# Windowed attention moved from VectorE products to masked band products on TensorE, beside a state-space scan, on one core

## Chip, cores and metric

One core of a Trainium2 chip. The metric is the time of one execution in microseconds (us): the median of the executions, lower is better. The profile's span, from the first to the last instruction, is about 2 us shorter than the time. Some executions fall into a slower state, over 1.5% above the fastest of the same kernel; ratios use fast ones alone, medians and ranges of times use all.

## The reference, cut to what matters

The output joins two independent halves, A and B, each for 2,048 positions and 448 features.

```python
def _A_ref(x, ...):                     # a diagonal complex recurrence over 2048 steps
    ...
    for t in range(L):
        h = Lam_bar[None, :] * h + Bu[:, t, :]
    ...
    y = 2.0 * jnp.einsum("blp,dp->bld", hseq, Cmat).real + x * Dskip

def _B_ref(x, wqkv, wo):                # 16 heads of 28; each query sees 8 keys, 2 apart
    qkv = (x @ wqkv).reshape(B, S, 3, H, Dh)...
    idx = pos[:, None] - jnp.arange(8) * 2          # masked where negative
    logits = jnp.einsum("bhsd,bhswd->bhsw", q, k[idx]) * Dh ** -0.5
    attn = softmax(logits)
    return jnp.einsum("bhsw,bhswd->bhsd", attn, v[idx]).reshape(B, S, D) @ wo
```

## The kernel before

Part A is untouched by the change: weights and transposes, a first level of products, a second level of seven steps, and a last phase of 16 steps (`coA`, `coB`, two evictions `ht`, `y_ps`, eviction `ya`). Part B before the change holds 16 positions in each of 128 partitions, so that a key 2w positions back lies in the same partition, and does the whole attention on VectorE.

```python
def prep(self):                                   # x is loaded plain and turned by TensorE
    for j in range(T):
        for k in range(KT):
            nc.tensor.transpose(pt[:, k, :], self.x_sb[:, j, k*KP:(k+1)*KP], self.ident[:])
        nc.scalar.copy(self.xT[:, :, j, :], pt[:])
    ...
def attention(self):
    for w in range(W):                            # scores: 8 products over 7168 elements, then sums
        V.tensor_tensor(pr[:], qd..., kd[:, :, off:off+T, :]..., op=ALU.mult)
        V.tensor_tensor(pr[:, 0:14], pr[:, 0:14], pr[:, 14:28], op=ALU.add)
        ...
    ...                                           # max, exp (ScalarE), sum, divide
    for (j0, j1) in ((0, 12), (12, 16)):
        for w in range(W):                        # values: product and sum
            V.tensor_tensor(tmp..., aa, vv, op=ALU.mult)
            V.tensor_tensor(acc..., acc..., tmp..., op=ALU.add)
        self.tail(j0, j1)                         # transposes, output projection, store
...
a.loads_params(); b.loads(); a.loads(); b.prep(); a.setup()
b.qk_proj(); b.v_proj(); a.setup_c(); a.setup_weights(); b.loads2()
a.main()                                          # TensorE, ScalarE
b.attention()                                     # VectorE: runs beside a.main()
```

## Time and profile before

| | before |
|---|---|
| time | 212.96 us, median of 2 (212.83 to 213.09) |
| span | 211.4 us |
| VectorE busy | 181.0 us (86%) |
| TensorE busy | 160.4 us (76%) |
| TensorE's granted clock, mean | 0.96 |

From the page of the kernel before: busy time of the engines (DVE is VectorE, PE TensorE), three rows of the span in 40 slices (each digit the busy share of 5.3 us in tenths; PEclk is the granted clock), and the shares of the chain that ended last.

```profile
PE 160.4 (76%) x1709; PEld 117.4 (56%) x1709; DVE 181.0 (86%) x197; ACT 100.2 (47%) x193; POOL 28.1 (13%) x35
PE   0004999999997799999995763998888883297773
DVE  0359998888929999999999996999999999999950
PEclk9999999999999999999999998599999999569999
PE 46%; DVE 33%; ACT 8%; DMA 6%; issue 3%; SPq 2%; ACTq 0%; DVEq 0%
```

VectorE is above 90% in nearly all slices from 63 us to the end, and TensorE is busy in the same slices. The chain runs through TensorE first and through VectorE after it.

The same kernel by stages. Columns: stretch in us, its length, then the busy time of TensorE, TensorE's weight loads, VectorE, ScalarE and GpSimd, the clock, the DMA share and GB/s.

```profile
18.50:62.60 44.10, 43.82 (x268) 25.64 (x269) 36.85 (x63) 20.76 (x35) 26.95 (x16) 1.00 0.54 137
123.70:176.80 53.10, 42.42 (x404) 28.02 (x401) 50.22 (x26) 27.56 (x55) 0.00 (x0) 0.94 0.31 90
176.80:211.40 34.60, 19.80 (x128) 11.42 (x128) 27.14 (x33) 8.52 (x16) 0.00 (x0) 0.85 0.17 57
```

From 18.5 us, when x has landed, to 62.6 TensorE does part B's projections without a hole. Part A's last phase, 123.7 to 176.8, lies wholly beside VectorE's softmax and value products (50.2 of 53.1 us busy). Only the 34.6 us after it are attention alone.

Two of the groups of VectorE instructions that the change removes (count, then busy us and mean ns of one):

```profile
L129 DVE TENSOR_TENSOR prod<-qd,kd 128x7168 bf16<-128x7168 bf16 x8 | 30.7, 3840 | 0.1
L165 DVE TENSOR_TENSOR pv_tmp<-attn,vd 128x5376 bf16<-128x5376 bf16 (+1 forms) x14 | 28.3, 2021 | 0.3
```

### The profile page before, as it was taken

What the parts mean: (1) busy time and instruction counts of PE and PEld (TensorE: products, weight loads), DVE (VectorE), ACT (ScalarE), POOL (GpSimd) and SP (SyncE); (2) the same over time, 40 slices, a digit from 0 to 9 for tenths busy, and PEclk for the clock granted to TensorE, in tenths of its full rate; (3) what the DMA queues carried; (4) which work ended last, traced back from release to release, by engine and by line L of the source; (5) the groups of instructions that cost most, each with busy time, mean ns of one, the idle gap of its engine ahead of it and who ended that gap; (6) DMA issues with size and microseconds to landing.
All of it is one profiled execution on the core that took longest, in us unless ns stands there. A gap on an engine that the chain in (4) does not pass through costs nothing.

```text
span 211.4 us, 4117 instructions
## 1 busy us (share of the span) xinstructions
PE 160.4 (76%) x1709; PEld 117.4 (56%) x1709; DVE 181.0 (86%) x197; ACT 100.2 (47%) x193; POOL 28.1 (13%) x35
## 2 busy tenths in 40 slices
PE   0004999999997799999995763998888883297773
PEld 0003765555567799999994652565555551154441
DVE  0359998888929999999999996999999999999950
ACT  2053792002689993344337796344455541024432
POOL 2000899991000000000000000000000000000000
PEclk9999999999999999999999998599999999569999
DMA  1599940485508515422231011134354411012212
GB/s 0 103 351 289 244 108 0 108 192 161 212 2 209 95 47 171 164 106 90 87 118 59 3 43 43 47 110 129 92 137 126 112 43 43 0 43 72 83 65 87
DMA packets 23836, 22.17 MB, mean 105 GB/s; under 512 B 11786, under 2 KB 23114, under 8 KB 23562
## 3 DMA queue, kind: packets, MB, share of 16 engines
q1 hardware_dynamic: 20231, 20.32, 32.9%
q10 hardware_dynamic: 3587, 1.59, 3.2%
q8 instruction: 13, 0.21, 0.5%
q14 instruction: 5, 0.04, 0.1%
HBM read 11.36 MB, written 7.34 MB: 88 GB/s over the span
## 4 chain that ended last, share of the span: by engine, by line
PE 46%; DVE 33%; ACT 8%; DMA 6%; issue 3%; SPq 2%; ACTq 0%; DVEq 0%
PE qkv_ps L95 18%; DVE pv_tmp L165 13%; DVE acc L167 10%; PE l1A L392 7%; DMA xb_sb<-in_B_x_dram 6%; PE l1B L392 5%; PE wo_ps L188 3%; PE pt_x L80 3%; DVE oT_sb L185 2%; PE pt_x L415 2%; DVE o_nat L169 2%; ACT Bcat L379 2%; PE l1A L397 1%; PE l1A L399 1%; ACT Ccat L250 1%
## 5 line engine op out<-in xcount | busy, mean ns | idle before, releaser
L95 PE MATMUL qkv_ps<-wqkv_p,xbT_sb 112*128 112x448 bf16 x192 | 40.1, 361 | 0.0
L129 DVE TENSOR_TENSOR prod<-qd,kd 128x7168 bf16<-128x7168 bf16 x8 | 30.7, 3840 | 0.1
L165 DVE TENSOR_TENSOR pv_tmp<-attn,vd 128x5376 bf16<-128x5376 bf16 (+1 forms) x14 | 28.3, 2021 | 0.3
L95 PEld LDWEIGHTS <-xbT_sb 112*128 112x128 bf16 x192 | 18.8, 100 | 15.5
L392 PEld LDWEIGHTS <-Bcat 112*128 112x128 bf16 x448 | 26.2, 98 | 0.0
L167 DVE TENSOR_TENSOR acc<-acc,pv_tmp 128x5376 bf16<-128x5376 bf16 (+1 forms) x12 | 24.3, 2024 | 0.3
L80 PE MATMUL pt_x<-ident,xb_sb 128*112 128x128 bf16 x64 | 7.8, 266 | 18.8 <-DMA xb_sb<-in_B_x_dram 18.5
L483 ACT CAST ya<-y_ps 128x448 bf16<-128x448 f32 x16 | 8.5, 531 | 23.4 <-issue 18.8
L191 ACT CAST yb<-wo_ps 128x448 bf16<-128x448 f32 x16 | 8.5, 532 | 23.3 <-PE wo_ps L188 23.3
L80 PEld LDWEIGHTS <-xb_sb 128*112 128x112 bf16 x64 | 7.5, 173 | 21.1 <-DMA xb_sb<-in_B_x_dram 18.5
L402 ACT CAST ht<-l1A 128x512 bf16<-128x512 f32 x16 | 9.4, 587 | 19.2 <-issue 17.0
L119 ACT CAST vd<-qkv_ps 128x448 bf16<-128x448 f32 x16 | 8.4, 536 | 20.8 <-PE qkv_ps L95 20.7
L392 PE MATMUL l1A<-xaT_sb,Bcat 112*128 112x128 bf16 x256 | 18.1, 219 | 0.0
L188 PE MATMUL wo_ps<-wo_p,oT_sb 112*128 112x448 bf16 x64 | 15.0, 382 | 3.8 <-DVE oT_sb L185 3.7
L131 DVE TENSOR_TENSOR prod<-prod 128x3584 bf16<-128x3584 bf16 x8 | 16.2, 2025 | 0.3
L343 POOL TENSOR_TENSOR Mmat<-Dm,Scat 128x896 bf16<-128x896 f32 x7 | 11.6, 1688 | 19.3 <-DVE Scat L335 19.3
L392 PE MATMUL l1B<-xaT_sb,Bcat 112*128 112x128 bf16 x192 | 14.2, 219 | 0.0
L81 ACT COPY xbT_sb<-pt_x 112x512 bf16<-112x512 bf16 x16 | 8.8, 587 | 7.3 <-PE pt_x L80 7.3
L184 PE MATMUL pt_o<-ident,o_nat 128*112 128x128 bf16 x64 | 5.8, 244 | 8.3 <-DVE o_nat L169 8.3
L113 DVE TENSOR_SCALAR qd<-qkv_ps 128x448 bf16<-128x448 f32 x16 | 10.0, 625 | 2.1
L188 PEld LDWEIGHTS <-oT_sb 112*128 112x128 bf16 x64 | 6.0, 103 | 10.1 <-DVE oT_sb L185 5.0
L469 PEld LDWEIGHTS <-ident 128*128 128x128 bf16 x112 | 11.3, 101 | 0.0
(206 smaller groups left out, 360.9 us busy)
## 6 DMA issues: line engine op xcount, KB each, us to landing
hs<-ht SPq DMA_DIRECT2D x16, 224.0 KB, 1.9
hin<-hs SPq DMA_DIRECT2D x16, 224.0 KB, 2.7
xb_sb<-in_B_x_dram SPq DMA_DIRECT2D x1, 1792.0 KB, 12.3
xa_sb<-in_A_x_dram SPq DMA_DIRECT2D x1, 1792.0 KB, 7.9
out_dram<-ya SPq DMA_DIRECT2D x16, 112.0 KB, 1.7
out_dram<-yb SPq DMA_DIRECT2D x16, 112.0 KB, 1.7
kd<-kd ACTq DMA_DIRECT2D x1, 1372.0 KB, 9.1
vd<-vd SPq DMA_DIRECT2D x1, 1372.0 KB, 9.4
```

Of the source, the lines that this page charges most:

```text
L80: nc.tensor.transpose(pt[:, k, :], self.x_sb[:, j, k * KP:(k + 1) * KP], self.ident[:])
L95: nc.tensor.matmul(ps[:].rearrange("p d h -> p (d h)"), lhsT=self.xT[:, k, j, :], rhs=self.wp[:, k * 3 + which].rearrange("p d h -> p (d h)"),
L113: V.tensor_scalar(self.qd[:, :, j, :], ps[:], scale, None, op0=ALU.mult)
L129: V.tensor_tensor(pr[:], qd[:].rearrange("p d j h -> p d (j h)"), kd[:, :, off:off + T, :].rearrange("p d j h -> p d (j h)"), op=ALU.mult)
L131: V.tensor_tensor(pr[:, 0:14], pr[:, 0:14], pr[:, 14:28], op=ALU.add)
L165: V.tensor_tensor(tmp[:, :, 0:n, :], aa, vv, op=ALU.mult)
L167: V.tensor_tensor(acc[:, :, j0:j1, :], acc[:, :, j0:j1, :], tmp[:, :, 0:n, :], op=ALU.add)
L188: nc.tensor.matmul(ps[:], lhsT=oT[:, kt, j, :], rhs=self.wo_p[:, kt, :], start=(kt == 0), stop=(kt == KT - 1))
L343: eng.tensor_tensor(out_tile, Dm[:].unsqueeze(1).unsqueeze(1).to_broadcast([NCH, n, 2, PL]), scal.unsqueeze(3).to_broadcast([NCH, n, 2, PL ...
L392: nc.tensor.matmul(reg(m), lhsT=self.Bcat[:, k, m, :], rhs=self.xT[:, k, j, :], start=(k == 0 and m in (0, MA)), stop=(not has_prev and k ...
L402: nc.scalar.copy(ht[:, 0:MA, :], psA[:])
L469: nc.tensor.matmul(reg(m), lhsT=ident[:], rhs=hin[:, m, :], start=(m in (0, MA)), stop=False, skip_group_check=True)
```

## The change

The intent: scores and values become matrix products on TensorE instead of VectorE's 135 us of products, which go. For 114 queries and the 128 keys that cover their windows, each head has one score matmul (28 rows, four heads at rows 0, 32, 64 and 96), an exp, a product with a 0/1 band mask, and one value matmul whose extra column of ones gives the softmax's denominator. x arrives already transposed, by four large DMA transposes on SyncE's queue. Of the eight PSUM tiles of the kernel before (6 and 2 in the diff's last lines) the two score tiles, of double size, take the room of four, so that all else has four instead of eight.

```diff
 def loads(self):
-    nc.sync.dma_start(self.x_sb[:], self.B_x[0].rearrange("(p j) d -> p j d", j=T))
+    for c in range(2):
+        nc.sync.dma_start_transpose(self.xT[:, 0:3, cols], self.B_x[0, rows, 0:384])
+        nc.sync.dma_start_transpose(self.xT[:, 3, cols], self.B_x[0, rows, 320:448])
 ...
+def qk_proj(self, c):                      # q and k transposed: four heads of 32 rows in a tile
+    for w in range(2):
+        for hg in range(4):
+            ...4 matmuls of 512 columns into qk_ps...
+            if n % 2 == 0: nc.scalar.copy(dst, ps[:])
+            else:          nc.vector.tensor_copy(dst, ps[:])
+def block(self, b):
+    for hg in range(4):
+        for h in range(4):
+            nc.tensor.matmul(sp[h // 2][...], lhsT=self.kT[32*h:32*h+DH, hg, kc:kc+NCH],
+                             rhs=self.qT[32*h:32*h+DH, hg, QB*b:QB*b+nq], ...)
+    for u in range(2):
+        nc.scalar.activation(pt[...], sv, ACT.Exp, scale=scale)
+        V.tensor_tensor(pt[...], pt[...], mask..., op=ALU.mult)
+    for h in range(4):
+        for hg in range(4):
+            nc.tensor.matmul(po[0:nq, 4*hg+h, 0:DH+1], lhsT=pts[h // 2][:, h % 2, hg, 0:nq],
+                             rhs=self.va[:, b, 4*hg+h, 0:DH+1], ...)
+    V.reciprocal(r[0:nq], po[0:nq, :, DH])
+    V.tensor_tensor(on[0:nq], po[0:nq, :, 0:DH], r..., op=ALU.mult)
+    ...4 transposes of on into tp (pt_o)...
+    V.tensor_copy(self.oT[:, :, QB*b:QB*b+nq], tp[:, :, 0:nq])
+def wo(self, t): ...4 matmuls of 448 columns (wo_ps), eviction yb on ScalarE, store...
 def attention(self):
-    ...all of the VectorE products...
+    for b in range(self.NB):               # 18 blocks
+        self.block(b)
+        while (done + 1) * NCH <= end:
+            self.wo(done); done += 1
 ...
-        return psum.tile(shape, dtype, name=name, tag=tag, bufs=(6 if tag == "mm" else 2))
+        return psum.tile(shape, dtype, name=name, tag=("s" if tag == "s" else "mm"),
+                         bufs=(2 if tag == "s" else 4))
-a.loads_params(); b.loads(); a.loads()
+b.loads(); a.loads_params(); a.loads()
-b.qk_proj(); b.v_proj()
+b.projections()
 a.main()
 b.attention()
```

## The prediction

> **What bounds the kernel now.** Span 211.4 us. The table of engines has VectorE busy 181 us (86%), TensorE 160 us (76%, pipelined). The chain of waits has three stretches: until 18.5 us only loads (x of part B); then TensorE leads (part B's projections until 62.6, part A's weights and transposes until about 77, level 1 until 110.5, level 2 until 122.4); from 124.7 to the end VectorE (softmax, value products and sums, output projection). Part A's last phase (16 steps of 2.85 us in the timeline, ending at 176.8) is hidden under VectorE. So part A and attention overlap now.
>
> **What the change does.** It removes VectorE's attention work (about 135 us by the groups of lines) and the TensorE transposes of B's x. It adds, per block of 114 queries (18 blocks): 16 score matmuls, two exps of 912 elements, two mask products, 16 value matmuls, normalisation, 4 transposes and about one output projection. The decisive point is the compiled order: except scores, exps and masks of the first two blocks (and scores of a third), all attention stands after all of part A, on TensorE, ScalarE and VectorE alike. VectorE will idle for over 100 us; the overlap is given up.
>
> **Costing.**
> - Start: [...] First matmul at about 14 us (before 18.5).
> - Projections: matmuls of 448 columns come every 0.19 us; 512 columns then 0.216. 128 x 0.216 + 72 x 0.19 = 41 us, plus 3 for cold clock and waits: end at 58 (before 62.6).
> - Part A: now 62.6 to 176.8, of which about 8 us was stalled behind the softmax exp. That goes; but all 16 x transposes now precede level 1 (4.5 us less overlap), and early exps with a table load sit in ScalarE's order (3 us). Estimate 115 us: end at 173.
> - Attention after it, per block: exps 2 x 0.9 us (2048 elements took 1.91, 512 from PSUM 0.59); masks 2 x 0.63 (1792 elements took 1.09, 5376 2.96); normalising 0.6, oT copy 0.42; output eviction 0.53; value matmuls 0.9; projection 0.76. No engine has over 3 us, but scores fill all four score banks, so the next scores wait for both exps, and stand in TensorE's order ahead of the output projection and the next value matmuls. Loop: value matmuls 0.9, last scores 0.2, wake 0.3, exps 1.75, next scores 0.55, projection 0.76: 4.4 us. Start 8, 15 x 4.4, tail 5: about 77 us, where before only the 35 us after 176.8 were exposed.
> - 58 + 115 + 77 = 250 us.
>
> **Predicted: 250 us, 8 in 10 between 235 and 268.** Faster by over 2%: 3%; within 2%: 3%; slower: 94%.
>
> **Shown right by:** VectorE near idle from about 60 to 172 us; no value matmul before part A's last y_ps; blocks 4 to 5 us apart with TensorE waiting for the exp, no engine over 75% busy there; the chain of waits alternating TensorE and ScalarE; first projection at 10 to 16 us.
>
> **Wrong if:** score matmuls of the four row groups overlap and a block takes 3.3 us or less (then about 232); the clock falls in the gaps of attention (blocks over 5.5 us); the DMA transposes hold the queue so that part A's parameters, and with them GpSimd's 27 us of matrix building, come late (up to 15 us more).

The sum is: 14 + 41 + 3 = 58 for the projections, and 58 + 115 + 77 = 250. The cold clock can be seen in the trace of the kernel before: until 25.1 us the transposes of 128 columns come every 0.107 us, after it every 0.056. A falling clock can be seen there too: 0.50 was granted from 130.9 to 137.8 us and from 178.7 to 189.0, each time after 4 us in which TensorE was busy for less than 1.6. A table load takes 1.28 us.

## The result, and the profile after

The kernel after takes 281.25 us (280.93 to 281.56, two executions), 1.321 times the time before (95% interval 1.317 to 1.326): slower, and above the range of 235 to 268. All outputs are right. Ratios here are the mean time of one kernel's fast executions over that of the other's in the same rounds, so not quite the ratio of the medians quoted.

| | before | after |
|---|---|---|
| time | 212.96 | 281.25 us |
| VectorE busy | 181.0 (86%) | 74.2 us (27%) |
| TensorE busy | 160.4 (76%) | 224.4 us (80%) |
| granted clock, mean | 0.96 | 0.81 |
| projections end | 62.6 | 74.0 us |
| part A ends | 176.8 | 184.8 us |
| attention after part A | 34.6 | 94.0 us |

The same lines of the page of the kernel after:

```profile
PE 224.4 (80%) x2234; PEld 155.2 (56%) x2237; DVE 74.2 (27%) x161; ACT 127.2 (46%) x221; POOL 33.4 (12%) x52
PE   0172957999998999996778888888998998988873
DVE  0104895343300100001000000025534536345321
PEclk9997877999999999999999999995555555555555
PE 51%; ACT 17%; DVE 13%; issue 9%; SPq 7%; DMA 2%; ACTq 0%
```

VectorE is empty for the middle third: the overlap is gone, as predicted. And the clock is 0.5 in the last 13 slices, which are the attention stage. There the same matmul takes twice as long (448 columns of the projection come every 0.37 us, where those of part A's last phase at full clock come every 0.19), and a good part of TensorE's longer busy time is that: a run below that keeps the clock for most of the stage (e3) has 198.8 us of it, although it streams more.

By stages, in the columns of the table before:

```profile
12.65:74.00 61.35, 49.16 (x202) 21.37 (x204) 29.60 (x65) 20.45 (x36) 26.95 (x16) 0.89 0.36 78
139.00:184.80 45.80, 39.47 (x399) 26.48 (x397) 0.00 (x0) 22.93 (x50) 0.00 (x0) 1.00 0.36 104
184.80:278.80 94.00, 76.75 (x668) 52.30 (x665) 40.06 (x86) 38.36 (x49) 0.00 (x0) 0.51 0.07 22
```

The prediction's sum was 58 + 115 + 77. The trace has 74.0 + 110.8 + 94.0 = 278.8: 16 us more, 4 less, 17 more.

**The start.** SyncE's queue, in order of time (start, length of the issue), the first and last of the four transposes and of part A's seven parameter loads:

```profile
0.73 8.25 SPq L67 DMA_TRANSPOSE xbT_sb<-in_B_x_dram  x1
...
15.74 1.30 SPq L68 DMA_TRANSPOSE xbT_sb<-in_B_x_dram  x1
17.09 0.72 SPq L218 DMA_DIRECT2D lre_raw<-in_A_Lambda_re_dram  x1
...
21.21 0.62 SPq L224 DMA_DIRECT2D dsk_raw<-in_A_Dskip_dram  x1
```

The parameters of part A, 0.9 KB each, stand behind 16.3 us of transpose issues and land at 20.5 to 25.6 us. VectorE's instruction order has their casts ahead of the projection's evictions. The waits that follow (who waited for whom: us in total, times, longest):

```profile
DVE lre L268 <- DMA lre_raw<-in_A_Lambda_re_dram: 11.5, 1, 11.5
PE qk_ps L109 <- DVE qT L119: 7.1, 1, 7.1
PE qk_ps L109 <- DVE v_aug L134: 4.9, 2, 2.7
```

TensorE fills its four PSUM tiles and waits 7.1 us for an eviction (`qT`) that VectorE can't start, because it waits for the parameters. The 4.9 us are two later holes. In them VectorE works through part A's tiny operations, and some of these are slow. VectorE and then GpSimd, in order of time:

```profile
33.80 1.66 DVE L342 CAST S1hi_bf<-Scat 128x14 bf16<-128x14 f32 x1
35.38 0.16 DVE L361 COPY gs<-g_re 128x7 f32<-128x7 f32 x1
```

```profile
32.09 4.99 POOL L348 TENSOR_TENSOR Mmat<-Dm,Scat 128x896 bf16<-128x896 f32 x3 [24.63 <-DVE Scat L340]
```

A cast of 128x14 elements takes 1.66 us, where the copy of 128x7 after it takes 0.16; GpSimd's three matrix products at the time take 1.66 us each. That the durations agree is all that the traces show; no run here tests whether GpSimd slows VectorE. From 12.65 to 74.0 TensorE is idle 61.35 − 49.16 = 12.2 us, and the 49.16 us busy are 8 more than the 41.3 that the matmuls take at full clock (128 x 0.216 + 72 x 0.19): the granted clock there is 0.5 for 13.7 us (mean 0.89), which explains at most 6.8 of the 8. Until 16.9 us, where the trace's records of the clock begin, the matmuls of 512 columns come every 0.43 us, and every 0.216 after it: up to 2 us more.

**The attention.** One block of the steady state, from the chain of waits in order of time (start, length, what; the pieces called "issue", of 0.02 to 0.05 us, left out):

```profile
203.03 1.49 PE o_ps L160 x16
204.54 0.27 DVE r L164
204.83 0.64 DVE o_nat L166
205.51 0.64 PE pt_o L170 x4
206.18 0.41 DVE oT L171
206.63 1.68 PE wo_ps L177 x4
```

A block takes 5.28 us: `wo_ps` 1.68, `o_ps` 1.49, `r` 0.27, `o_nat` 0.64, `pt_o` 0.64, `oT` 0.41. Neither the exp nor the scores are in it. The prediction's loop through four score banks and two exps (4.4 us) is not the one that binds. The loop goes through the output projection, because `wo_ps` of a block needs `oT` of the same block and stands in TensorE's order before the next block's value matmuls. And every matmul in it runs at half clock: 448 columns in 0.42 or 0.37 us, where part A's last phase takes 0.19 a piece.

### The profile page after: what moved, and what is told of

The parts are those of the page before. It is cut to its first block, busy times and chain, and to the rows that moved or that the text cites. A ratio compares the mean times of both kernels' runs of the same rounds, so it can differ in the third digit from the quotient of the medians.

```text
span 278.8 us, 5182 instructions
## 1 busy us (share of the span) xinstructions
PE 224.4 (80%) x2234; PEld 155.2 (56%) x2237; DVE 74.2 (27%) x161; ACT 127.2 (46%) x221; POOL 33.4 (12%) x52
## 4 chain that ended last, share of the span: by engine, by line
PE 51%; ACT 17%; DVE 13%; issue 9%; SPq 7%; DMA 2%; ACTq 0%
PE wo_ps L177 10%; PE o_ps L160 9%; PE qk_ps L109 7%; SPq L67 4%; PE l1A L397 4%; PE pt_o L170 4%; DVE o_nat L166 4%; PE v_ps L129 4%; PE y_ps L482 3%; PE l1B L397 3%; ACT xaT_sb L421 3%; ACT ya L488 2%; DVE oT L171 2%; DVE r L164 2%; DMA dsk_raw<-in_A_Dskip_dram 2%
## 5 line engine op out<-in xcount | busy, mean ns | idle before, releaser
L109 PE MATMUL qk_ps<-xbT_sb,wqk_p 128*128 128x512 bf16 x125 | 36.0, 447 | 24.8 <-DMA xbT_sb<-in_B_x_dram 12.7
L109 PEld LDWEIGHTS <-wqk_p 128*128 128x128 bf16 x128 | 14.1, 110 | 45.6 <-issue 35.3
L153 ACT ACTIVATE pt<-s_ps 128x912 bf16<-128x912 f32 (+1 forms) x36 | 33.2, 931 | 7.7 <-PE s_ps L145 5.0
L154 DVE TENSOR_TENSOR pt<-pt,mask 128x912 bf16<-128x912 bf16 (+1 forms) x36 | 22.4, 622 | 53.4 <-ACT pt L153 53.1
L160 PEld LDWEIGHTS <-pt 128*114 128x114 bf16 (+1 forms) x288 | 30.6, 210 | 5.6 <-issue 5.6
L160 PE MATMUL o_ps<-v_aug,pt 128*114 128x29 bf16 (+1 forms) x288 | 29.0, 249 | 0.0
L177 PE MATMUL wo_ps<-wo_p,oT 112*128 112x448 bf16 x64 | 26.8, 574 | 2.5 <-DVE oT L171 1.5
L170 PE MATMUL pt_o<-ident,o_nat 114*112 114x114 bf16 (+1 forms) x72 | 11.1, 307 | 10.4 <-DVE o_nat L166 10.3
L145 PE MATMUL s_ps<-qT,kT 28*128 28x114 bf16 (+1 forms) x288 | 17.9, 271 | 0.8 <-ACT pt L153 0.7
L129 PE MATMUL v_ps<-wqkv_nat,xbT_sb 128*128 128x448 bf16 x72 | 14.3, 352 | 0.0
L397 PE MATMUL l1B<-xaT_sb,Bcat 112*128 112x128 bf16 x192 | 13.3, 219 | 0.0
```

Of the source, the lines that this page charges most:

```text
L109: nc.tensor.matmul(ps[:], lhsT=self.wp[:, w, k, 4 * hg:4 * hg + 4].rearrange("p h d -> p (h d)"), rhs=self.xT[:, k, self.XP + 512 * c:self ...
L129: nc.tensor.matmul(ps[:].rearrange("p h d -> p (h d)"), lhsT=self.xT[:, k, c0:c0 + NCH], rhs=self.wn[:, k, 2 * D:3 * D], start=(k == 0), s ...
L145: nc.tensor.matmul(sp[h // 2][:, h % 2, QB * hg:QB * hg + nq], lhsT=self.kT[32 * h:32 * h + DH, hg, kc:kc + NCH], rhs=self.qT[32 * h:32 * ...
L153: nc.scalar.activation(pt[:, :, :, 0:nq], sv, ACT.Exp, scale=scale)
L154: V.tensor_tensor(pt[:, :, :, 0:nq], pt[:, :, :, 0:nq], self.mask[:, 0:nq].unsqueeze(1).unsqueeze(1).to_broadcast([NCH, 2, 4, nq]), op=ALU ...
L160: nc.tensor.matmul(po[0:nq, 4 * hg + h, 0:DH + 1], lhsT=pts[h // 2][:, h % 2, hg, 0:nq], rhs=self.va[:, b, 4 * hg + h, 0:DH + 1], start=Tr ...
```

## The experiments

The expectations name theories by letters:
- A: the parameters behind the transposes make the holes in the projections.
- B: the clock falls because too few columns stream in the attention's blocks. B'' (rival): only the value matmuls matter, since their 29 columns take 0.024 us at half clock (an estimate from 448 in 0.37) and their weight load 0.21 (its mean in the page of after). B3 (formed later): once lost, the clock comes back only after some 3.4 us of nearly unbroken streaming (in the table of windows below it came back after 13 windows of 3.41 us, 0.86 to 1.00 full).
- C: the block's chain runs through the `oT` copy and the output projection, not through the exps.
- D: the lost overlap is what costs most.
- E: projection evictions on VectorE are held up by part A's small operations.
- F: with attention beside part A, waits of a block stand in TensorE's order ahead of part A's matmuls.

Kernels that ran together ran on the same chip and share the executions of the kernel before, whose medians were 211.6 to 212.9 us.

### The start: e1_params_act, e2_params_first, e7_act_evict

e1 moves the parameter loads to ScalarE's queue:

```diff
-    nc.sync.dma_start(raw[0:PL], v)
+    nc.scalar.dma_start(raw[0:PL], v)        # likewise the other halves and dsk
```

> The changed kernel with one thing moved: the seven tiny parameter loads of part A are issued from ScalarE's queue instead of SyncE's, where they stood behind four DMA transposes (queue busy 0.7 to 17.0 us). Theory A (the transposes hold the queue, the parameters land late, and VectorE, which takes its instructions in order, can't free the projections' PSUM tiles until then): the hole of 7.1 us in TensorE at 19.3 us goes, the projections end at 58 to 64 us instead of 74, total 281 down to 265 to 272. Rival A' (the projections are slow for their own reasons: cold clock, late second half of x[...]): end of the projections moves by less than 4 us and the total stays above 276.

Measured: 284.5 us, ratio 1.340 (1.335 to 1.346). A miss: slower than the kernel after. ScalarE's queue in order of time, the second half of `lim`, the first of `ldt`, and `dsk`:

```profile
5.97 0.60 ACTq L219 DMA_DIRECT2D lim_raw<-in_A_Lambda_im_dram  x1
13.24 0.60 ACTq L218 DMA_DIRECT2D ldt_raw<-in_A_log_dt_dram  x1
17.80 0.35 ACTq L224 DMA_DIRECT2D dsk_raw<-in_A_Dskip_dram  x1
```

The issues stand still from 6.6 to 13.24 us and from 14.5 to 17.8. TensorE's first matmul, which waits for the first transpose, starts at 13.3 us, so the first of these waits ends about when that transpose lands; what the issues waited for is not shown. `dsk` landed at 26.5 us. The hole in the projections grew to 9.7 us. So "another queue" was not the cure; theory A itself was not tested by it.

e2 puts the parameters ahead of the transposes on the same queue:

```diff
-b.loads(); a.loads_params()
+a.loads_params(); b.loads()
```

> The changed kernel with the old order on the SyncE queue: the seven parameter loads first, then the four transposes. Theory A: x lands about 4.4 us later (first matmul at about 17 instead of 12.7 us) but VectorE is never blocked on parameters; projections end at 62 to 67 us, total 268 to 275. Rival A': 74 + 4 us, total about 285.

Measured: 275.2 us, ratio 1.296 (1.291 to 1.302); 6 us better than after. The parameters land by 12.5 us and the 7.1 us hole is gone, although the first matmul now starts at 16.9 us. The projections end at 68.5, a little later than the 62 to 67 expected. A hole of 5.1 us at 28.1 to 33.2 stays, in which VectorE does this:

```profile
27.59 0.16 DVE L331 TENSOR_SCALAR sB<-g_im 64x7 f32<-64x7 f32 x1
27.77 3.17 DVE L332 COPY sB<-g_im 64x7 f32<-64x7 f32 x1
...
32.50 1.27 DVE L119 CAST kT<-qk_ps 128x512 bf16<-128x512 f32 x2
```

A copy of 64x7 elements takes 3.17 us, where the line above does 64x7 in 0.16. In the traces of before and after the same copy takes 3.17 us too, from 23.3 and from 38.0, and beside it, from the same moment, a product on GpSimd takes 3.19. In e2 the eviction `kT` stands behind the copy.

e7 is e2 with all projection evictions on ScalarE:

```diff
-if n % 2 == 0:
+if True:                                   # ScalarE for q, k; the same for v
```

> Parameters first on the SyncE queue (275 us as measured) plus all evictions of the projections on ScalarE, none on VectorE. Theory E (with the parameters early, what still holes the projections is that their evictions stand in VectorE's order behind part A's small setup copies[...]): the hole of 5 us at 28 to 33 us goes, projections end at 60 to 64 us instead of 68.6, total 267 to 271. Rival E' (cold clock, x still landing): end within 2 us of 68.6, total 273 to 276.

Measured: 269.0 us, ratio 1.265 (1.260 to 1.270). Projections end at 62.1 us instead of 74.0, all 12 us of it in the time. Theories A and E are shown as far as the order of instructions goes: 12 of the 16 us that the first term was short come back, although x arrives 4 us later, when the parameters are early and no eviction stands behind VectorE's small operations. That GpSimd is what slows these is a guess from their durations and was not tested.

### The clock: e3_wide, e3b_order, e3c_wide2

e3 lets each value matmul stream up to four heads' columns (128) instead of 29. The surplus goes to columns that later matmuls overwrite, so heads go in rising order and the result is right.

```diff
-for h in range(4):
-    for hg in range(4):
-        matmul(po[0:nq, 4*hg+h, 0:DH+1], ..., rhs=self.va[:, b, 4*hg+h, 0:DH+1])
+for hg in range(4):
+    for h in range(4):
+        hh = 4*hg + h; nh = min(4, H - hh)
+        matmul(po[0:nq, hh:hh+nh, :], ..., rhs=self.va[:, b, hh:hh+nh, :])
```

> The changed kernel; each value matmul streams the ones-augmented values of four heads (up to 128 columns) instead of 29, heads in rising order so that later heads overwrite the unwanted columns (right result). No wait is removed and no gap of TensorE closed; only more columns stream through the array per weight load. Theory B (the granted clock of 0.50 in the attention follows from how few columns stream there, about 4500 per 5.3 us): the clock returns to 1.0 in the attention, the 16 value matmuls take about 0.9 instead of 1.5 us and the output projection 0.8 instead of 1.5 us, blocks 3.6 to 4.2 us apart instead of 5.28, total 255 to 264. Rival B' (the gaps of 0.5 to 0.9 us or the mixture of small tiles set the clock): clock stays at 0.50, value matmuls 1.5 to 1.8 us, total 281 to 287.

Measured: 259.1 us (255.9 to 259.9), ratio 1.216 (1.206 to 1.225): four times the value work, and 22 us faster. e3b changes the order of heads alone, e3c streams 64 columns.

> Control for the run with wide value matmuls: the changed kernel with its 29 columns, only the heads taken in the rising order that the wide version needed. Theory B (streamed columns set the clock): clock stays at 0.50 in the attention, total 279 to 284. If it comes down towards 259, the order did it and theory B falls.

> As the wide run but with the values of two heads (64 columns) per value matmul: about 500 more streamed columns a block instead of 1400. Theory B as a matter of degree: the clock falls earlier than in the wide run (there at about 230 us, after some ten blocks) or doesn't stay up at all, total 262 to 282. If 64 columns hold the clock as well as 128 (total below 259), the amount of streaming is not what decides, rather passing some small floor.

Measured: 280.7 us, ratio 1.327, and 281.6 us, ratio 1.330; both as after. The clock rows of the pages of e3 and e3c, 40 slices of the span each:

```profile
PEclk9997798999999999999999999999999999985597
```

```profile
PEclk9996877999999999999999999996555555555555
```

With 128 columns the clock stays near full but for two slices near the end; with 64, or in another order, it is 0.5 for the whole stage (e3b's row is as e3c's). e3's profiled execution was slow, 1.6% above its fastest. The stage after part A took 74 us in it, 94 in after: in this order of instructions the clock is worth 20 us, more than the 17 by which the prediction's attention was short.

### The chain: e4_wo_later, e4b_wide_later

e4 does a block's output projection one block later; e4b adds e3's wide value matmuls.

```diff
-end = min(S, self.QB * (b + 1))
+end = min(S, self.QB * b)                  # and the rest after the last block
```

> The changed kernel; the output projection of 128 rows is emitted one block later, so that it no longer waits for the transposed output of the block just computed. Theory C (the loop that closes a block is value matmuls, reciprocal, normalising, transposes, copy, output projection, next value matmuls, 5.28 us at half clock): the copy and its waits (0.4 to 0.8 us a block) leave the loop, blocks 4.4 to 4.8 us apart at half clock, total 266 to 274; if the smaller gaps also bring the clock back (rival B'), 3.2 to 3.8 us and a total of 250 to 257. Rival C' (the exps and the four score banks close the loop, as the prediction had it): blocks stay within 0.2 us of 5.28.

> The changed kernel with both edits that worked on the attention: value matmuls of up to 128 columns and the output projection one block later. If the streamed columns set the clock (theory B) and the loop of waits sets the period (theory C), the two gains add: clock 1.0 through the attention, blocks 2.9 to 3.3 us apart (value matmuls 0.9, reciprocal 0.3, normalising 0.6, transposes 0.3, projection 0.8), total 242 to 252. If the clock falls again partway as in the run with wide value matmuls alone (it fell at about 230 us, at the one block without a projection), 252 to 258.

Measured: e4 271.0 us, ratio 1.280 (1.271 to 1.289), blocks of 4.61 us still at clock 0.50. e4b 245.9 us, ratio 1.157 (1.151 to 1.163), blocks of 3.03 us at full clock throughout. In e4's chain of waits a block is `wo_ps` 1.49, `o_ps` 1.49, `r` 0.27, `o_nat` 0.64, `pt_o` 0.63: `oT` has left it, and 0.67 us a block went with it. That is theory C. The exp is still not in the chain, in e4b either.

### What the clock follows: f1_twice, f3_thrice, f4_wide_start

f1 and f3 compute the output projection two and three times (the last one counts), which adds nothing but streaming; f4 makes the value matmuls wide in the first four blocks only.

```diff
-for k in range(KT):                        # output projection
+for k in 2 * tuple(range(KT)):             # f1; f3: 3 *
 ...
-nh = min(4, H - hh)                        # e3
+nh = min(4 if b < 4 else 1, H - hh)        # f4
```

> The changed kernel with useless work added: every output projection is computed twice into the same tile (8 matmuls of 448 columns instead of 4; the result stays right). Theory B (the clock follows from how much streams through the array): the added 1792 columns a block bring the clock to 1.0, so although TensorE gets 64 more matmuls the blocks shrink from 5.28 to 4.0 to 4.6 us and the total falls to 255 to 270. Rival B'' (what mattered were value matmuls no shorter than their weight load): clock stays 0.50, blocks grow by 1.5 us to 6.8, total 300 to 308.

Measured: 303.5 us, ratio 1.429. The clock stayed at 0.50 but for one stretch of 3.4 us (233.6 to 237.0). Theory B, as I had put it, fell: more streaming at half clock did not bring the clock back.

> The output projection of each block is computed three times instead of once (two of the three are useless; the result is right): 12 matmuls of 448 columns in one row, an estimate of 4.5 us at the half clock from the 1.49 us of four. Theory B3 (once lost, the clock comes back only after about 3.4 us of nearly unbroken streaming): the clock returns during the attention stage, and the kernel is faster than the one with the projection twice (303.5) although it does more: 270 to 295. Rival B'' (only the value matmuls' width matters, streaming elsewhere is worth nothing): clock 0.50 to the end, blocks of about 8.3 us, 325 to 335.

Measured: 298.3 and 298.4 us in the two fast executions, 307.2 and 308.0 in two slow ones (median of all 302.8). The number missed B3's range of 270 to 295, yet the fast executions are 5 us faster than f1 with one projection more per block, and far from the 325 to 335 of B''. From f3's stages, 192 to 195 us (columns as before; the clock is the last but two):

```profile
192.00:193.00 1.00, 1.00 (x5) 0.34 (x3) 0.00 (x0) 0.00 (x0) 0.00 (x0) 0.50 0.00 0
193.00:194.00 1.00, 1.00 (x6) 0.51 (x5) 0.00 (x0) 0.00 (x0) 0.00 (x0) 0.89 0.00 0
194.00:195.00 1.00, 1.00 (x19) 0.90 (x16) 0.00 (x0) 0.57 (x2) 0.00 (x0) 1.00 0.00 0
```

TensorE is busy without a gap from 190 to 193.2, and then the clock is back at 1.00. It was lost again at 223.9, back at 234.2, and from there it changes at 237.6, 244.4, 247.8, 251.2, 254.7, 258.1, 261.5 and so on to the end: always multiples of 3.41 us apart. Theory B'' falls, since the value matmuls are as narrow as ever.

> Value matmuls of 128 columns in the first four blocks of 114 queries, of one head (32 columns) in the rest. If only the passage into the attention stage decides (a clock that is held there stays): full clock to near the end, blocks of about 3.7 us, 255 to 263, as with wide value matmuls everywhere (259). If the steady state with narrow value matmuls can't hold the clock: it falls to 0.50 within one or two blocks of the fourth, and the time is 270 to 281.

Measured: 278.3 us, ratio 1.302 (1.296 to 1.308). The same of f4:

```profile
193.00:194.00 1.00, 1.00 (x19) 0.97 (x19) 0.00 (x0) 0.06 (x1) 0.00 (x0) 0.66 0.00 0
201.00:202.00 1.00, 1.00 (x13) 1.00 (x11) 0.00 (x0) 0.53 (x1) 0.00 (x0) 0.50 0.00 0
```

The clock is lost at 190.3, returns at 193.7 in the wide part, is lost for good at 200.5, and the narrow steady state never brings it back. So it is not only the passage into the stage.

Where a trace has several changes of the clock (e3, f1, f3, f4, and before and after, from 23.75 us on in the latter), all lie multiples of 3.41 us apart. So I cut each trace into windows of 3.41 us on the grid of its own changes and counted, for every window, the columns that stream in it: each matmul's columns laid end to end from its start, at the measured rate (448 columns in 0.189 us at full clock and in 0.373 at 0.50, estimates of 8,090 and 4,100 in 3.41 us), scores at a quarter, since four run side by side (in after, from 188.23 us, four start within 0.01 us and the next four 0.095 later, the time of one at half clock), transposes in full. Over the attention stages of after, e3, e3b, e3c, e4, f1, f3 and f4:

| clock in the window, and in the next | windows | columns streamed | share of what the clock could stream |
|---|---|---|---|
| full, stays full | 23 | 3,608 to 6,004 | 0.45 to 0.74 |
| full, falls | 20 | 449 to 3,498 | 0.06 to 0.43 |
| half, returns | 13 | 3,541 to 4,107 | 0.86 to 1.00 |
| half, stays half | 159 | 0 to 3,494 | 0.00 to 0.85 |

One count orders all of these windows: about 3,500 columns. After fewer the next window ran at half clock, after more at full, whatever the clock in the window itself. At full clock 3,500 is 0.43 of what could stream, at half clock 0.85, and so in these runs a clock once lost was hard to get back. This is a reading after the fact, and no run was made for it, but the twelve other traces test it. From part A's last phase on they have 355 windows: all with 3,526 columns or more were followed by full clock, all with 2,982 or fewer by half, and none lay between. From the end of the projections on, the 20 traces have 1,060: the 761 with 3,500 or more were followed by full clock, the 271 below 3,180 by half, and the 28 between went either way, so the count is good to about a tenth. (A window of nothing but part A's transposes, 3,584 columns from 81.8 us in after, was followed by full clock, so transposes count. In the projections some matmul records are missing from most traces, so the count is not made there.)

One block streams 1,792 columns in the projection, 448 in the transposes, 456 in the scores and 464 in the values, 3,160 in all. At full clock a block of after would take 3.7 us (e3's shorter blocks), an estimate of 2,900 columns per window: the clock falls. The same estimate gives 3,400 for e3c, which falls, 4,200 for e3 with its 1,856 value columns, which holds with one lapse, 4,450 for f3 (blocks of 5.16 us), which holds for a time, and 5,100 for e4b (3.03 us), which holds. The mean is not enough, since windows of one kernel differ. e4 (at e4b's 3.03 us) and f1 (at an estimated 4.46) would have 3,560 and 3,790, but both lost the clock on entering the stage, in windows of 1,984 and 1,376 columns. At half clock f1's windows then reached at most 3,494, until one of 3,541 brought the clock back at 233.6; the next window had too few and it was lost again. So in these runs the amount of streaming tells when the clock fell, as theory B had it; what fell with f1 is the idea that adding streaming to a block is enough.

### The overlap: e5_co, e8c_best, e9a_split, e9b_split_all

e5 makes the attention a generator and calls one block after each of part A's 16 last steps, with the projection one block later as in e4.

```diff
-    a.main()
-    b.attention()
+    step = b.attention_steps()             # yields after each block
+    a.main(step)                           # calls next(step) after each ya of the last phase
+    for _ in step: pass
```

> The changed kernel, attention emitted one block after each of the 16 steps of part A's last phase, output projection one block later; nothing else differs, start and projections stay as slow as in the changed kernel. Theory D (most of the loss is that the attention stands after part A, where before it ran beside it): steps of the last phase grow from 2.85 to 4.4 to 4.8 us, TensorE filled, clock 1.0; attention after part A shrinks from 94 to about 10 us; total 218 to 230. Rival D' (the masked band products are simply too much work for TensorE at the clock they get): the clock falls in the mixed steps too, steps of 6 us or more, total above 245.

Measured: 246.1 us, ratio 1.149 (1.140 to 1.158); two executions, the profiled one among them, were slow. That is above the range of theory D, and as slow as rival D' said, but not for its reason: the clock is 1.00 in the mixed steps, 139 to 220 us. A step takes 5.81 us, not the 4.4 to 4.8 expected. One step of the chain (pieces under 0.3 us left out):

```profile
163.43 1.50 PE y_ps L490 x7
165.12 0.82 PE o_ps L160 x16
166.26 0.64 DVE o_nat L166
166.94 0.41 PE pt_o L170 x4
167.35 0.77 PE wo_ps L177 x4
168.15 0.53 ACT yb L181
168.68 0.51 ACT ht L486
```

The block and part A's step don't overlap, they alternate in one chain: `y_ps`, the block's values, two VectorE operations, transposes, projection, ScalarE's evictions `yb` and `ht`, `y_ps`. In the trace TensorE runs its matmuls in the order of the program: while `pt_o` waits for `o_nat` (0.76 us idle before 166.94), no matmul of part A runs. That is theory F.

e8c adds e7's help for the start, moves half of part A's evictions to VectorE, and puts two blocks into level 2.

> All together, to see whether the masked band products can beat the old kernel: parameters first, projection evictions on ScalarE, attention blocks beside part A's last phase (two of them in level 2), output projection one block later, and half of part A's evictions on the now idle VectorE. Sum by theories A, C, D, E: projections end 62, then 11 + 36 + 14 us to the last phase, 16 x 4.5 us, tail 6: 203 us, range 195 to 212 (ratio to the old kernel 0.92 to 1.00). If the clock falls in the mixed phase, 225 or more.

Measured: 228.5 us, ratio 1.074 (1.067 to 1.080), far above the 195 to 212 expected; the steady steps are still 5.81 us.

e9a is e5 with the block cut in parts, so that part A's matmuls lie between what a block issues and what it waits for; e9b has all helps and the cut.

```diff
-def block(self, b): ...                    # scores, exps, values, o_nat, pt_o, oT
+def scores(self, b): ...   # after the previous block's pt_o: scores, exps, masks
+def values(self, b): ...   # between part A's evictions and its y_ps: values, r, o_nat
+def finish(self, b): ...   # after y_ps: pt_o, oT; then the next scores, then wo of the block before
```

> As the run with attention blocks beside part A's last phase (246 us, steps of 5.81 us), but each block is cut so that its waits fall behind part A's matmuls: value matmuls between the evictions and y, transposes after y, scores of the next block one step early. Theory F (those steps were long because reciprocal, normalising and evictions stood in TensorE's order with nothing beside them, not because of work or clock): TensorE's own work is 0.8 + 0.9 + 1.55 + 0.25 + 0.35 + 0.76 = 4.6 us a step, steps 4.5 to 5.0, total 228 to 235. Rival F' (ScalarE and VectorE or the four general PSUM tiles limit it): steps stay above 5.4, total above 240.

> All that helped: parameters first, projection evictions on ScalarE, half of part A's evictions on VectorE, the cut blocks beside part A's last phase and two of them in level 2. By theory F 16 x 1.1 us less than the 228 us of the run with all together: 208 to 215, ratio to the old kernel 0.97 to 1.01. This is the test of whether the band products can beat the old kernel here.

Measured: e9a 236.0 us, ratio 1.112 (1.107 to 1.118), steady steps of 5.36 us; e9b 215.9 us, ratio 1.019 (1.012 to 1.026). Both lie just above their expected ranges, and e9a's steps above the 4.5 to 5.0. By the ratios the cut is worth 8 us in e9a (1.149 to 1.112) and 12 in e9b (1.074 to 1.019). TensorE's busy share in the mixed steps goes from 0.83 in e5 to 0.96 in e9a. In e9b TensorE is busy 77.9 of the 80 us from 125 to 205 at a clock of 1.00. So theory D holds in kind: against e4, which has the later projection alone, the overlap is worth 28 us in e5 and 36 in e9a by the ratios, more than the clock's 20 or the start's 12, though part of it is again the clock, which holds in the mixed steps.

### The rest of the start: e10_chunk, e11_early, e11p_early

e10 puts the first half of x ahead of the parameters and the second after them; e11 also loads part A's x early and transposes it before the last quarter of the projections; e11p is e11 with the parameters first.

```diff
 def loads(self):                           # e10
-    for c in range(2): ...transposes of chunk c...
+    self.load_x(0)                         # and load_x(1) after a.loads_params()
 for c in range(4):                         # e11, projections
+    if c == 3: a.transpose_x()
```

> As the 216 us version, but only the second half of x's transposes stands behind the parameter loads; the first half stands ahead of them. First matmul at 12.7 instead of 17 us; some of it is lost again because ScalarE, which now evicts the projections, waits for parameters until about 20 us. Total 211 to 216.

> As the run before, plus part A's x loaded early into a tile of its own and transposed before the last quarter of the projections, evicted by both engines, so that it no longer stands between the projections and level 1 (13 us there for about 9 us of TensorE work). Total 207 to 213; if it stays within 1 us of the run before, that stretch was TensorE's own work.

> The same early transposes of part A's x on the version with all parameters first (216 us): 211 to 214. It tells which order of the start is better with the rest equal.

Measured: e10 217.8 us, ratio 1.024 (1.019 to 1.028), a miss, with no gain over e9b's ratio. Its first matmul starts at 13.4 us instead of 17.0, but TensorE then waits 5.3 us for evictions on ScalarE, which waits 16.5 us for the parameters, and the projections end at 65.2 instead of 62.8. e11 212.3 us (211.8 to 216.9, the last a slow one), ratio 0.999 (0.994 to 1.004): the kernel before's time. e11p 214.8 us, ratio 1.012 (1.006 to 1.017). These two do not tell which order of the start is better: in both traces the projections end at 65.2 us and level 1 at 108.1, and the difference comes in and just after level 2, where e11p's clock was at half for two windows and e11's for none. The page of e11:

```profile
PE 185.5 (88%) x2234; PEld 134.0 (64%) x2237; DVE 86.6 (41%) x189; ACT 115.6 (55%) x193; POOL 33.4 (16%) x52
PEclk9999699999999999999999999999999999999999
```

TensorE is busy 88% of the span, VectorE 41%. This is the best version found, and it does not beat the kernel before: it has turned a VectorE bound of 181 us into a TensorE bound of 186.

## Why the prediction was wrong

The direction was right and the size was not: 281.25 against 250, above the range.

- **"the overlap is given up"**: right. VectorE is busy 0.00 us from 139 to 184.8, no value matmul starts before 184.8, and e5 and e9a, which put the overlap back and move the projection one block later, are 28 and 36 us faster by the ratios than e4, which only moves the projection (in part because the clock holds beside part A's matmuls).
- **"Estimate 115 us" for part A**: right in size, 110.8 measured.
- **"about 14 us" for the first matmul**: right, 12.65. It starts when the first transpose, 0.79 MB, has landed, at 12.61 us. With 1.2 MB of weights and other loads beside it, the DMA engines moved 202 GB/s until then.
- **"plus 3 for cold clock and waits: end at 58"**: the first step that failed. The work of 41.3 us was right; cold clock and waits took 20 (12.2 idle, and 8 more busy, of which the granted half clock explains at most 6.8 and the slow start up to 2) instead of 3, and the projections ended at 74.0. The prediction named the late parameters as a danger, but charged them to GpSimd's matrix building. The runs show another way: VectorE's order puts the parameters' casts, and small operations that ran long beside GpSimd (1.66 and 3.17 us), ahead of the evictions that TensorE needs (e2 gained 6 us, e7 6 more).
- **"scores fill all four score banks, so the next scores wait for both exps … 4.4 us"**: the second step, wrong in kind. The exps are in no chain of a steady block, and TensorE, for which "no engine over 75% busy" was said, is busy 82% of the stage. The loop is values, normalisation, transposes, `oT`, projection; moving the projection shortened it (e4, e4b).
- **"Start 8, 15 x 4.4, tail 5: about 77 us"**: wrong in size, 94 measured, because the durations put in were those at full clock. The stage ran at 0.50. "The clock falls in the gaps of attention (blocks over 5.5 us)" was listed as a way to be wrong, and the clock did fall, with blocks of 5.28 us, at 187.6 us and after no long gap: in the 3.41 us before, TensorE's longest idle was 0.69. At nearly full clock with the same order (e3) the stage took 74 us, by chance close to 77.
- **"score matmuls of the four row groups overlap"**, listed as a way to be too slow: they do. Ten take 0.46 us at half clock, where one of 114 columns would take 0.094 by itself (an estimate from 448 in 0.37). It gained nothing, because scores are not in the chain.

The sum: −1.4 (first matmul) + 17.4 (projections) − 4.2 (part A) + 17 (attention) over 250 is 278.8, the span; the time of the profiled execution is 2.1 us longer.

Left open: the count of columns behind the clock is read off traces, and no run was built to test it; what makes VectorE's small operations slow was not tested, nor what held e1's loads on ScalarE's queue; wide value matmuls were not tried together with e11, where the clock is full anyway; and why f3 has two times was not followed.

## What to carry to other kernels

Here moving the work of the busiest engine to another cost 32% of the time, and nothing (e11, 0.999) once the new engine's order interleaved it with what used to run beside it and the start was mended. In these traces TensorE ran its matmuls in program order, so cut the new stage where it waits and put the other stage's matmuls there. Cost a stage of short matmuls by the columns that stream in each 3.41 us at full clock: where windows in these traces had fewer than about 3,500 (0.43 of what could stream), the matmuls took twice the time from there on (448 columns 0.37 us instead of 0.19). Put tiny loads that other work waits for ahead of large DMA transposes (the four held their queue for 16.3 us in after; e2 gained 6 us; but e10 and e9b, without evictions on VectorE, show no gain in either order), and keep evictions that TensorE waits for off an engine with a string of small operations in front of them (e7 gained 6 more).
